# A decode block on one core: TensorE's loop from seven turns over two places of 64 KB to nine turns over three places of 32 KB

## The chip, the core and the metric

The kernel runs on one core of a Trainium2 chip. A core has five engines that run side by side and meet only at semaphores: TensorE (PE in the profile) multiplies matrices, VectorE (DVE), ScalarE (ACT) and GpSimd (POOL) do the work between the products, and SyncE (SP) here only issues transfers. Sixteen DMA engines move data from the chip's memory (HBM) to the core's own memory (SBUF: 128 partitions); products come out in PSUM, in eight banks. The metric is the device time of one execution in microseconds (us), less is better.

## What is computed

One decode step of a transformer block, in float32, for 8 sequences of one token each: attention over the last 1024 positions of a cache, then a gated MLP. Cut to what matters (`layernorm` has no gain; `B_x` is not used):

```python
x = A_x                                              # (8, 1, 1024)
q = layernorm(x) @ wq                                # 32 heads of 128; wq is 1024 x 4096
k, v = the last W = 1024 rows of k_cache, v_cache    # (8, 4 heads, 1024, 128), each for 8 query heads
p = softmax(q k^T / sqrt(128))
h = x + (p v) @ wo                                   # wo is 4096 x 1024
g, u = layernorm(h) @ w_gate, layernorm(h) @ w_up    # 1024 x 3584
out = h + (gelu(g) * u) @ w_down                     # 3584 x 1024
```

Every weight and every cached row is used once, so 111 MB have to come from HBM for some 0.1 MB of activations.

## The kernel before

The weights and the cache are packed ahead of the launch so that each transfer reads one long row for each of the 128 partitions. They come as 13 **passes** (`PASSES`, line 25): `q0 q1` (the query projection), `k0 v0 k1 v1` (keys and values of sequences 0 to 3 and 4 to 7), `o0 o1` (output projection), `g0 u0 g1 u1` (gate and up projection, in a part of 2048 and one of 1536 columns) and `d0` (16 of the 28 row chunks of the down projection). A full pass is 16384 words for each partition, 64 KB; `g1` and `u1` have 12288.

SBUF tile `w` has two **places** of 64 KB (`HALF`), and pass *i* goes to place *i* mod 2. `load` (line 225) issues the transfers on SP's queue, in the passes' order. The transfer of a pass waits until TensorE is through with the pass two before it, which had the same place, so while one pass is multiplied the next one is on its way. `d0` comes as two transfers of 32 KB. Behind it come the 12 remaining row chunks of the down projection, in transfers of 7, 2 and 2 chunks (`PARTS`; 4096 bytes a chunk and partition) and the last chunk cut into 640 and 384 words.

TensorE runs a real loop of seven turns (lines 168 to 182). A turn holds a pass from place 0 (`one_pass(0)`), eight transposes of `p_sb` (the softmax; in most turns their result is not used), and a pass from place 1; the last turn holds `d0` alone. In a pass a chunk `c` of 128 rows is multiplied by four products, one for each 32 columns of the array (line 161): the stationary operand is a 128 x 32 piece of `st[s]` (activations, 1024 columns a place), the moving one 128 x 512 words of `w`. Chunks 0 to 3 add up in one PSUM bank, 4 to 7 in the next. The profile has two records for each of these products. Behind the loop stand 16 products for 8 row chunks of the down projection (line 202), 12 for the next three (line 209), and 8 for the last chunk (line 217).

Between the passes the other engines fold the partial sums, run the softmax and the norms, and write the activations of the next pass into `st`. TensorE waits for a transfer (`s_la`, `s_lh`, `s_lb`) and for an activation (`s_ta`, `s_tb`) with separate semaphores. VectorE's whole program is recorded and then put in a block that is run once; ScalarE, GpSimd and SP run straight through. The order of everything is the order in which it is written.

Of the kernel before, what the change touches and what calls it, by code (L numbers as in the profile page):

```python
# [4 lines left out]
AF = mybir.ActivationFunctionType  # L5
# [3 lines left out]
P = 128  # L9
# [11 lines left out]
HALF = 16384  # L21
# [5 lines left out]
PASSES = ("q0", "q1", "k0", "v0", "k1", "v1", "o0", "o1", "g0", "u0", "g1", "u1", "d0")  # L27
TURNS = 7

FIRST = 16  # L30
PARTS = (7, 2, 2)

QUADS = 24
# [74 lines left out]
def decode_block(nc, out, x, srcs, W):  # L108
# [3 lines left out]
    def sb(name, shape):  # L112
# [9 lines left out]
    s_x0, s_x, s_la, s_lh, s_lb, s_ta, s_tb, s_p, s_at, s_id = [  # L122
        nc.alloc_semaphore("s_" + n) for n in ("x0", "x", "la", "lh", "lb", "ta", "tb", "p", "at", "id")]
# [4 lines left out]

    w = sb("w", [P, 2 * HALF])
    st = [sb(f"st{s}", [P, D + 32]) for s in range(2)]  # L130
    p_sb = sb("p", [P, W])
    ident = sb("ident", [P, P])
    at_ = sb("at", [P, DF // P, 32])
# [10 lines left out]
    tail_at = []  # L144
    at = HALF
    for n in PARTS:
        tail_at.append(at)
        at += n * D
    last_at = at
# [5 lines left out]
    def one_pass(s):  # L155
        for c in range(NC):
            if s == 0 and c == 4:
                take(s_lh, 16)
            for j in range(NQ):
                at = s * HALF + ((c // 4 * NQ + j) * 4 + c % 4) * N  # L160
                ins = nc.tensor.matmul(  # L161
                    bank(2 * s + c // 4)[32 * j:32 * j + 32, :],
                    st[s][:, (c * NQ + j) * 32:(c * NQ + j + 1) * 32], w[:, at:at + N],
                    start=(c % 4 == 0), stop=(c % 4 == 3))
        ins.then_inc(pe.sem, 1)

    nc.tensor.wait_ge(s_id, 1)
    with nc.Fori(0, TURNS, 1, engines=on_pe, hint_back_edge=True) as turn:
        take(s_la, 16)
        take(s_ta, 1)  # L170
        one_pass(0)
        with nc.tensor.If(turn < TURNS - 1):
            take(s_p, 1)
            for h in range(2):
                for i in range(KC // 2):
                    c = h * KC // 2 + i
                    ins = nc.tensor.transpose(pp[h][:, i], p_sb[:, c * P:(c + 1) * P], ident)  # L177
                ins.then_inc(pe.sem, 1)
            take(s_lb, 16)
            take(s_tb, 2)  # L180
            one_pass(1)

    def done(name):
        t, s = divmod(PASSES.index(name), 2)
        return (pe.sem, 4 * t + (4 if s else 1))

    def turned(t, h):
        return (pe.sem, 4 * t + 2 + h)

    pe.n = 4 * (TURNS - 1) + 1  # L190

    rows = DF // P
    place, of = [], []
    for i, n in enumerate(PARTS):
        for k in range(n):
            place.append(tail_at[i] + k * D)
            of.append((s_dn[i], 16))
    for q in range(FIRST, QUADS):
        for ch in range(2):
            r = 2 * (q % 2) + ch  # L200
            at = place[q - FIRST] + ch * N
            ins = pe(lambda e: e.matmul(  # L202
                bank(6)[32 * r:32 * r + 32, :], at_[:, q, :], w[:, at:at + N],
                start=(q < FIRST + 2), stop=(q >= QUADS - 2)), of[q - FIRST], (s_at, 1), inc=False)
    t_pairs = pe.mark(ins)
    for q in range(QUADS, rows - 1):
        for j in range(NQ):
            at = place[q - FIRST] + j * QW
            ins = pe(lambda e: e.matmul(  # L209
                bank(7)[32 * j:32 * j + 32, 0:QW], at_[:, q, :], w[:, at:at + QW],  # L210
                start=(q == QUADS), stop=(q == rows - 2)), of[q - FIRST], inc=False)
# [37 lines left out]
    for name in PASSES[:-2]:  # L249
        next_load(name)  # L250
# [320 lines left out]
```

## Time and profile before

| | us |
|---|---|
| time, median of 3 runs | 265.15 (265.07 to 265.83) |
| the profiled execution, its own time | 265.19 |
| its span, from the first to the last instruction | 263.9 |
| outside the span | 1.3 |
| TensorE busy | 132.7 |
| VectorE, ScalarE, GpSimd busy | 37.3, 19.1, 4.4 |
| read from HBM | 111.18 MB, 422 GB/s over the span |

The profile is of one execution. Times are counted from the start of the span. A share of the DMA engines is that of all 16, and a row of short stretch can read above 1, since a packet's whole time is put to where it starts. "PEclk" is TensorE's granted clock: 1.00 is 2.4 GHz, 0.50 is 1.2 GHz.

### The profile page before, as it was taken

Reading aid. Unit: us, or ns where it says so; the run is one execution under the profiler, and the core shown is the slowest. Engines: PE = TensorE matmul, PEld = TensorE weight load, DVE = VectorE, ACT = ScalarE, POOL = GpSimd, SP = SyncE. Lnnn points to the kernel's source line nnn. Section 1 sums busy time; section 2 is a strip of 40 time slices with the busy share of each in tenths; the row PEclk is TensorE's granted clock in tenths of the full one; section 3 lists DMA queues with packets and bytes.
Section 4 is the critical chain, followed back from the end, with each engine's and each line's share of the span. In section 5 each row is a group of like instructions: output and inputs, shape, how many; then the busy total and the mean of one; then the engine's idle time right before and its main releaser. Section 6 shows DMA issues by size and latency. Waiting matters only on the chain. (4 is left out here: it accounts for less than half of the span.)

```text
span 263.9 us, 2184 instructions
## 1 busy us (share of the span) xinstructions
PE 132.7 (50%) x952; PEld 41.6 (16%) x952; DVE 37.3 (14%) x105; ACT 19.1 (7%) x28; POOL 4.4 (2%) x11
## 2 busy tenths in 40 slices
PE   0004905806826507618608509409509187683766
PEld 0001301201222102112102202002203022220222
DVE  0060110120120200120220100540100301012013
ACT  1030000000020000100000000210300002010000
POOL 2000100000000000000000000000000001000000
PEclk9999975985956965975957956956968959799579
DMA  8997999999899979998998999799989989999993
GB/s 318 482 457 338 477 477 397 397 477 467 348 457 477 457 338 477 477 407 387 477 477 358 437 477 457 338 477 477 447 375 410 477 380 454 397 467 407 417 422 137
DMA packets 3073, 111.33 MB, mean 422 GB/s; under 512 B 480, under 2 KB 768, under 8 KB 896
## 3 DMA queue, kind: packets, MB, share of 16 engines
q1 hardware_dynamic: 2880, 111.20, 97.9%
q10 hardware_dynamic: 192, 0.11, 0.1%
q8 instruction: 1, 0.02, 0.0%
HBM read 111.18 MB, written 0.13 MB: 422 GB/s over the span
## 5 line engine op out<-in xcount | busy, mean ns | idle before, releaser
L161 PE MATMUL banks<-w,st 128*32 128x512 f32 x832 | 118.4, 731 | 120.3 <-PEq L153 120.3
L161 PEld LDWEIGHTS banks<-w,st 128*32 128x32 f32 x832 | 33.0, 131 | 200.7 <-issue 200.7
L177 PE MATMUL banks<-ident,p 128*128 128x128 f32 x48 | 7.4, 303 | 6.3 <-PEq L153 6.3
L177 PEld LDWEIGHTS banks<-ident,p 128*128 128x128 f32 x48 | 5.8, 154 | 11.5 <-issue 11.5
L354 ACT ACTIVATE p<-banks,nmax 128x1024 f32<-128x1024 f32 x2 | 2.2, 1114 | 73.3 <-DVE nmax L90 73.3
L90 DVE TENSOR_REDUCE nmax<-banks 128x1 f32<-128x1024 f32 x2 | 2.4, 1224 | 33.9 <-PE banks L161 33.9
L90 DVE TENSOR_TENSOR y_sum<-y_sum,banks 128x512 f32<-128x512 f32 (+1 forms) x4 | 2.1, 552 | 33.0 <-PE banks L161 18.1
L202 PE MATMUL banks<-w,at 128*32 128x512 f32 x32 | 5.3, 829 | 2.1 <-DMA w<-weights 2.1
L90 DVE TENSOR_SCALAR q<-banks 128x512 f32<-128x512 f32 x2 | 1.4, 692 | 31.1 <-PE banks L161 31.1
L90 DVE TENSOR_TENSOR us<-us,banks 128x512 f32<-128x512 f32 (+1 forms) x2 | 1.4, 685 | 30.4 <-ACT us L409 17.5
L90 DVE TENSOR_TENSOR o_sum<-o_sum,banks 128x512 f32<-128x512 f32 x2 | 1.4, 688 | 30.0 <-ACT o_sum L370 30.0
L90 DVE TENSOR_TENSOR gs<-gs,banks 128x512 f32<-128x512 f32 (+1 forms) x2 | 1.4, 686 | 27.5 <-ACT gs L412 14.2
L90 DVE TENSOR_TENSOR d_sum<-d_sum,banks 128x256 f32<-128x256 f32 (+1 forms) x3 | 1.4, 507 | 19.0 <-ACT d_sum L442 13.4
L370 ACT COPY o_sum<-banks 128x512 f32<-128x512 f32 x2 | 1.2, 585 | 27.7 <-PE banks L161 27.7
L409 ACT COPY gs<-banks 128x512 f32<-128x512 f32 (+1 forms) x2 | 1.2, 583 | 27.4 <-PE banks L161 27.4
L409 ACT COPY us<-banks 128x512 f32<-128x512 f32 (+1 forms) x2 | 1.2, 583 | 26.7 <-PE banks L161 26.7
L286 ACT ACT_TABLE_LOAD x2 | 2.6, 1283 | 1.9 <-DVE x_sb L90 1.9
L390 POOL COPY y_ex<-y_sum 64x256 f32<-64x256 f32 x1 | 0.4, 391 | 136.2 <-DVE y_sum L90 136.2
L202 PEld LDWEIGHTS banks<-w,at 128*32 128x32 f32 x32 | 1.6, 143 | 6.0 <-issue 6.0
L309 ACT COPY st<-ln_t 128x1024 f32<-128x1024 f32 x2 | 2.1, 1046 | 5.1 <-DVE ln_t L90 5.1
L90 DVE STREAM_TRANSPOSE at<-hm 32x128 f32<-32x128 f32 (+2 forms) x5 | 2.2, 440 | 0.1
L90 DVE SCALAR_TENSOR_TENSOR o<-o_sum,share,o 128x128 f32<-128x128 f32 x6 | 2.1, 352 | 0.2
(59 smaller groups left out, 38.3 us busy)
## 6 DMA issues: line engine op xcount, KB each, us to landing
w<-weights SPq DMA_DIRECT2D x2, 6144.0 KB, 22.1
w<-weights SPq DMA_DIRECT2D x2, 4096.0 KB, 18.9
w<-weights SPq DMA_DIRECT2D x1, 3584.0 KB, 18.8
w<-weights SPq DMA_DIRECT2D x2, 1024.0 KB, 22.5
w<-weights SPq DMA_DIRECT2D x1, 320.0 KB, 24.2
w<-weights SPq DMA_DIRECT2D x1, 192.0 KB, 24.2
w<-weights SPq DMA_DIRECT2D x10, 29.3
out<-o_fin ACTq DMA_DIRECT2D x1, 80.0 KB, 1.6
```

Source lines behind the costliest of these rows:

```text
L90: ins = getattr(self.eng, n.name)(*n.args, **n.kw)
L161: ins = nc.tensor.matmul(bank(2 * s + c // 4)[32 * j:32 * j + 32, :], st[s][:, (c * NQ + j) * 32:(c * NQ + j + 1) * 32], w[:, at:at + N], ...
L177: ins = nc.tensor.transpose(pp[h][:, i], p_sb[:, c * P:(c + 1) * P], ident)
L202: ins = pe(lambda e: e.matmul(bank(6)[32 * r:32 * r + 32, :], at_[:, q, :], w[:, at:at + N], start=(q < FIRST + 2), stop=(q >= QUADS - 2)) ...
L286: t = act(lambda e: e.activation(sd, ve, AF.Sqrt), t_ve)
L309: nc.scalar.copy(to[1], wide).then_inc(s_tb, 2)
L354: t = act(lambda e: e.activation(p_sb, bank(0, 2), AF.Exp, bias=nmax, accum_out=tot), t)
L370: t = dve(lambda e: e.tensor_add(o_sum, o_sum, bank(3)), act(lambda e: e.copy(o_sum, bank(2)), done(f"v{hb}")))
L390: t1 = pool(lambda e: e.tensor_copy(ex[64:P], far[0:64]), t)
L409: t = act(lambda e: e.copy(out[:nb], bank(b)[:nb]), ready)
```

## The change

The 13 passes become 27 **units** (`UNITS`) of four chunks each: what was one pass is now part 0 and part 1, and `d0` has three parts, that is 24 of the 28 row chunks. `w` has three places of 32 KB (`RING`, `UNIT`), and unit *u* goes to place *u* mod 3. The transfer of unit *u* waits for the products of unit *u* - 3. The loop has nine turns of three units, 48 products, with the eight transposes between the first and the second unit in every turn, and no branch inside. The four row chunks behind the loop have places of their own; they come in transfers of 2 and 1 chunks and, as before, 640 and 384 words.

One semaphore for each place (`s_in`) now counts both the 16 increments of a transfer and one "token" of the engine that filled `st`. `st` has three tiles of 512 columns. The order of the units isn't that of the passes everywhere: `k1` part 0 comes before `v0`, part 1 behind it (its first scores are put aside in `s1`), and `g1` part 0 comes before `u0` part 1. GpSimd takes over the clearing of `x_sb`, two additions and the copies for `d0`.

```diff
+UNITS = (
+    ("q0", 0), ("q0", 1), ("q1", 0),
+    ("q1", 1), ("k0", 0), ("k0", 1),
+    ("k1", 0), ("v0", 0), ("v0", 1),
+    ("k1", 1), ("v1", 0), ("v1", 1),
+    ("o0", 0), ("o0", 1), ("o1", 0),
+    ("o1", 1), ("g0", 0), ("g0", 1),
+    ("u0", 0), ("g1", 0), ("u0", 1),
+    ("g1", 1), ("u1", 0), ("u1", 1),
+    ("d0", 0), ("d0", 1), ("d0", 2),
+)
+RING = 3
+TURNS = len(UNITS) // RING
+UNIT = 4 * NQ * N
...
-PARTS = (7, 2, 2)
-
-QUADS = 24
+PAIRED = 24
+PARTS = (2, 1)
...
+    def unit(p):
+        take(s_in[p], 17)
+        for c in range(4):
+            if p == RING - 1 and c == 2:
+                take(s_half, 16)
             for j in range(NQ):
...
+    with nc.Fori(0, TURNS, 1, engines=on_pe, hint_back_edge=True):
+        unit(0)
+        take(s_p, 1)
+        for h in range(2):
+            for i in range(KC // 2):
+                c = h * KC // 2 + i
+                ins = nc.tensor.transpose(pp[h][:, i], p_sb[:, c * P:(c + 1) * P], ident)
+            ins.then_inc(pe.sem, 1)
+        unit(1)
+        unit(2)
...
+    def load(u):
+        p = u % RING
+        if u >= RING:
+            sp.wait(count(u - RING))
+        to = w[:, p * UNIT:(p + 1) * UNIT]
+        src = srcs[u]
+        if u == len(UNITS) - 1:
+            for k, sem in enumerate((s_in[p], s_half)):
+                n = UNIT // 2
+                nc.sync.dma_start(to[:, k * n:(k + 1) * n], src[:, k * n:(k + 1) * n]).then_inc(sem, 16)
             return
         n = src.shape[1]
...
+        if p == RING - 1 and n < UNIT:
+            to = to.rearrange("p (h n) -> p h n", h=2)[:, :, 0:n // 2]
+            src = src.rearrange("p (h n) -> p h n", h=2)
+        else:
+            to = to[:, 0:n]
+        nc.sync.dma_start(to, src).then_inc(s_in[p], 16)
...
+        if hb == 0:
+            scores, ready = bank(at_unit("k0", 0) % RING, 2), done("k0", 1)
+        else:
+            scores, ready = s1, act(lambda e: e.copy(s1[:, N:2 * N], bank(0)), done("k1", 1))
...
+    t = dve(lambda e: e.tensor_add(y_sum, y_sum, bank(1)), t, done("o0", 1))
+    t = dve(lambda e: e.tensor_add(y_sum, y_sum, bank(2)), t, done("o1", 0))
     h_sb = sb("h_sb", [P, QW])
...
+    t_h = folded("y", y_sum, (t, done("o1", 1)), h_sb, bank(0))
+    normed_in = layernorm_t(h_sb, "ln2", t_h)
+    normed_in(dve, "g0", 0)
+    normed_in(act, "g0", 1)
+    normed_in(act, "u0", 0)
...
+    t = pool(lambda e: e.tensor_add(d_sum[:, 0:QW], d_sum[:, 0:QW], h_sb), t)
+    t = dve(lambda e: e.tensor_add(d_sum, d_sum, bank(1)), t, done("d0", 1))
     pre = sb("pre", [P, QW])
...
+    t = folded("d", d_sum, (t, done("d0", 2)), pre, bank(2))
     t_pre = dve(lambda e: e.tensor_add(pre, pre, bank(7)[:, 0:QW]), t, t_quads)
```

How the instructions stand, first on TensorE from the last branch of the loop on. `s_dn0` to `s_dn4` are the transfers of the last row chunks, in their order; 32x512 is one product of 512 columns. Before:

```order
L168 COMPARE_AND_BRANCH
L202 MATMUL banks<-w,at 32x512 [waits s_dn0,s_at]
L202 MATMUL banks<-w,at 32x512 x13
L202 MATMUL banks<-w,at 32x512 [waits s_dn1]
L202 MATMUL banks<-w,at 32x512
L209 MATMUL banks<-w,at 32x256 x4
L209 MATMUL banks<-w,at 32x256 [waits s_dn2]
L209 MATMUL banks<-w,at 32x256 x7
L217 MATMUL banks<-w,at 32x160 [waits s_dn3]
L217 MATMUL banks<-w,at 32x160 x3
L217 MATMUL banks<-w,at 32x96 [waits s_dn4]
L217 MATMUL banks<-w,at 32x96 x3
```

And now, from the last unit of a turn on:

```order
L175 MATMUL banks<-w,st 32x512 [waits s_in2]
L175 MATMUL banks<-w,st 32x512 x7
L175 MATMUL banks<-w,st 32x512 [waits s_half]
L175 MATMUL banks<-w,st 32x512 x7
L181 REGISTER_ALU
L181 COMPARE_AND_BRANCH
L222 MATMUL banks<-w,at 32x256 [waits s_dn0]
L222 MATMUL banks<-w,at 32x256 x7
L222 MATMUL banks<-w,at 32x256 [waits s_dn1]
L222 MATMUL banks<-w,at 32x256 x3
L230 MATMUL banks<-w,at 32x160 [waits s_dn2]
L230 MATMUL banks<-w,at 32x160 x3
```

Behind the loop there are 36 products before and 20 now (the last four, of 96 columns, are cut off here); behind the third transfer from the end stand eight products of 256 columns before, four now.

On SP's queue stand the transfers of the weights; 128x16384 is 64 KB for each partition, `s_pe` the count of finished products. Before, from the third transfer on:

```order
L237 DMA w<-weights 128x16384 [waits s_pe] x8
L237 DMA w<-weights 128x12288 [waits s_pe] x2
L233 DMA w<-weights 128x8192 [waits s_pe]
L233 DMA w<-weights 128x8192
L258 DMA w<-weights 128x7168 [waits s_pe]
L258 DMA w<-weights 128x2048 x2
L258 DMA w<-weights 128x640
L258 DMA w<-weights 128x384
```

And now, from the fourth on:

```order
L255 DMA w<-weights 128x8192 [waits s_pe] x16
L255 DMA w<-weights 128x6144 [waits s_pe]
L255 DMA w<-weights 128x8192 [waits s_pe]
L255 DMA w<-weights 128x6144 [waits s_pe] x2
L255 DMA w<-weights 128x2x3072 [waits s_pe]
L255 DMA w<-weights 128x8192 [waits s_pe] x2
L247 DMA w<-weights 128x4096 [waits s_pe]
L247 DMA w<-weights 128x4096
L265 DMA w<-weights 128x2048
L265 DMA w<-weights 128x1024
L265 DMA w<-weights 128x640
L265 DMA w<-weights 128x384
```

With the first ones, that are not shown, 19 transfers become 32, of the same words in all, and the transfers of the last chunks no longer have a wait of their own.

## Rows read from the trace of the kernel before

**Rows 1.** The page: span, busy time by engine, and the weights' DMA queue.

```profile
span 263.9 us, 2184 instructions
...
PE 132.7 (50%) x952; PEld 41.6 (16%) x952; DVE 37.3 (14%) x105; ACT 19.1 (7%) x28; POOL 4.4 (2%) x11
...
q1 hardware_dynamic: 2880, 111.20, 97.9%
```

**Rows 2.** TensorE's timeline: start, us from start to end, line, shape, records [idle before].

```profile
23.15 8.49 PE L161 MATMUL banks<-w,st 128*32 128x512 f32 x64 [23.15 <-PEq L153]
...
61.84 9.62 PE L161 MATMUL banks<-w,st 128*32 128x512 f32 x64 [10.29 <-PEq L153]
...
177.95 9.59 PE L161 MATMUL banks<-w,st 128*32 128x512 f32 x64 [10.32 <-PEq L153]
...
197.30 8.45 PE L161 MATMUL banks<-w,st 128*32 128x512 f32 x64 [8.74 <-PEq L153]
211.83 9.71 PE L161 MATMUL banks<-w,st 128*32 128x512 f32 x64 [6.08 <-PEq L153]
...
226.36 8.77 PE L161 MATMUL banks<-w,st 128*32 128x512 f32 x64 [3.79 <-PEq L153]
236.07 3.64 PE L161 MATMUL banks<-w,st 128*32 128x512 f32 x32 [0.94 <-PEq L153]
245.64 6.44 PE L161 MATMUL banks<-w,st 128*32 128x512 f32 x32 [5.93 <-PEq L153]
254.16 5.34 PE L202 MATMUL banks<-w,at 128*32 128x512 f32 x32 [2.08 <-DMA w<-weights]
...
260.10 1.07 PE L209 MATMUL banks<-w,at 128*32 128x256 f32 x16 [0.18 <-DMA w<-weights]
260.99 0.62 PE L217 MATMUL banks<-w,at 128*32 128x160 f32 x16
```

**Rows 3.** The chain that ended last, its last pieces: start, us, what.

```profile
236.03 24.03 DMA w<-weights
...
260.10 1.11 PE banks L209 x16
...
261.24 0.43 DVE pre L90
...
261.93 0.25 DVE o_fin L90
```

**Rows 4.** The DMA view of 257.5 to 258.0: queue, packets, MB, share of 16 engines.

```profile
q8 instruction: 1, 0.02, 13.4%
```

**Rows 5.** Stretches of the tail: busy (count) by engine, PEclk, DMA share, GB/s.

```profile
254.00:256.00 2.00, 1.84 (x12) 0.61 (x16) 0.00 (x0) 0.00 (x0) 0.00 (x0) 0.69 1.02 426
256.00:258.00 2.00, 2.00 (x16) 0.72 (x12) 0.00 (x0) 0.00 (x0) 0.00 (x0) 0.50 1.00 411
258.00:259.00 1.00, 1.00 (x16) 0.40 (x12) 0.00 (x0) 0.00 (x0) 0.00 (x0) 0.92 0.96 370
259.00:260.00 1.00, 0.93 (x16) 0.17 (x6) 0.45 (x2) 0.00 (x0) 0.00 (x0) 1.00 0.36 126
260.00:261.00 1.00, 0.90 (x18) 0.56 (x21) 0.73 (x2) 0.41 (x1) 0.40 (x1) 1.00 0.05 17
```

**Rows 6.** VectorE's timeline: the second softmax, and the fold and norm behind `o1`.

```profile
109.65 1.23 DVE L90 TENSOR_REDUCE nmax<-banks 128x1 f32<-128x1024 f32 x1 [16.77 <-PE banks L161]
...
113.46 0.69 DVE L90 COPY st<-banks 128x512 f32<-128x512 f32 x1 [0.55 <-PE banks L177]
...
167.69 1.47 DVE L90 TENSOR_TENSOR y_sum<-y_sum,banks 128x512 f32<-128x512 f32 x3 [18.15 <-PE banks L161]
...
174.26 0.69 DVE L90 COPY st<-ln_t 128x1024 f32<-128x1024 f32 x1
```

**Rows 7.** The DMA view: issue of the second part of the output, KB, us to landing.

```profile
out<-o_fin SPq DMA_DIRECT2D x1, 48.0 KB, 1.6
```

More of the change, by code (lines that the diff above doesn't have):

```diff
@@ L165, in one_pass @@
         ins.then_inc(pe.sem, 1)
[L167 to L181, printed above, removed]
@@ L194, in decode_block, with count, done, turned @@
+    def count(u):
+        t, p = divmod(u, RING)
+        return (pe.sem, 5 * t + (1, 4, 5)[p])
+    def done(name, part):
+        return count(UNITS.index((name, part)))
+    def turned(u, h):
+        return (pe.sem, 5 * (u // RING) + 2 + h)
+    def token(u, ins):
+        ins.then_inc(s_in[u % RING], 1)
+    def at_unit(name, part):
+        return UNITS.index((name, part))
+    pe.n = 5 * TURNS
+    at = RING * UNIT
+    tail_at, place, of = [], [], []
     for i, n in enumerate(PARTS):
+        tail_at.append(at)
@@ L195, in decode_block @@
         for k in range(n):
-            place.append(tail_at[i] + k * D)
+            place.append(at + k * D)
             of.append((s_dn[i], 16))
[L198 to L201, printed above, removed]
+        at += n * D
+    for q in range(PAIRED, rows - 1):
+        for j in range(NQ):
+            k = place[q - PAIRED] + j * QW
             ins = pe(lambda e: e.matmul(
-                bank(6)[32 * r:32 * r + 32, :], at_[:, q, :], w[:, at:at + N],
-                start=(q < FIRST + 2), stop=(q >= QUADS - 2)), of[q - FIRST], (s_at, 1), inc=False)
@@ L205, in decode_block @@
[L205 to L211, printed above, removed]
+                bank(7)[32 * j:32 * j + 32, 0:QW], at_[:, q, :], w[:, k:k + QW],
+                start=(q == PAIRED), stop=(q == rows - 2)), of[q - PAIRED], inc=False)
@@ new lines, in queries_in @@
+    def queries_in(name, part):
+        u, hb = at_unit(name, part), int(name[1])
+        to = st[u % RING][:, 0:HB * 136].rearrange("p (b n) -> p b n", b=HB)
+        for hf in range(2):
+            ins = dve(lambda e: e.tensor_copy(
+                to[:, :, 64 * hf:64 * hf + 64].rearrange("p b (r n) -> p b r n", r=2)[:, :, :, 0:REP],
+                qt[hf][:, :, HB * hb:HB * hb + HB, 0].rearrange("p (r h) b -> p b r h", r=2)),
+                t_qt, t_zero[u % RING], inc=False)
+        token(u, ins)
@@ new lines, in decode_block, with lower, upper, let @@
+    gs, us, ge, hm = [[sb(f"{n}{k}", [P, N]) for k in range(2)] for n in ("gs", "us", "ge", "hm")]
+    def lower(out, name):
+        return act(lambda e: e.copy(out[:nb], bank_of(name, 0)[:nb]), done(name, 0))
+    def upper(out, name, t):
+        return dve(lambda e: e.tensor_add(out[:nb], out[:nb], bank_of(name, 1)[:nb]), t, done(name, 1))
+    def let(name, part, *deps):
+        for d in deps[:-1]:
+            pool.wait(d)
+        token(at_unit(name, part), nc.gpsimd.wait_ge(*deps[-1]))
@@ L441, in decode_block @@
+    chunks_in(1, t_u1)
+    t_us = upper(us[1], "u1", t_u1)
+    t = dve(lambda e: e.tensor_mul(hm[1][:nb], ge[1][:nb], us[1][:nb]), t_ge, t_us)
+    n = (rows - FIRST) * 32
+    t = dve(lambda e: e.transpose(at_[0:nb, FIRST:rows].rearrange("p c m -> p (c m)"), hm[1][:nb, 0:n]), t)
+    for j in range(NQ - 1):
+        c = FIRST + 4 * j
+        t = dve(lambda e: e.transpose(
+            at_[nb:P, c:c + 4].rearrange("p c m -> p (c m)"), hm[1][32 * j:32 * j + 32, n:N]))
+    chunks_in(2, t)
     d_sum = sb("d_sum", [P, N])
-    t = act(lambda e: e.copy(d_sum, bank(0)), done("d0"))
```

276 lines of the change are left out of this document (115 added, 161 removed).

## The prediction

> **What bounds the kernel now.** I read the page first: the span is 263.9 us, TensorE is busy for half of it, and the one queue that brings the weights fills the 16 DMA engines for 97.9% [rows 1]. Then TensorE's timeline: from pass to pass its bursts start 19.35 us apart (61.84 to 177.95 is 116.11 us for six passes), whatever the burst itself takes, and before each it has been idle for 4 to 10 us [rows 2]. So the transfers set the pace, and a burst starts when its data land. Last the chain that ended last: 24.03 us of DMA up to 260.06, then 1.11 us of products, VectorE's additions to 262.18, and the output [rows 3]. The end is thus the landing of the third transfer from the end, at 260.06, plus 3.8 us.
>
> How did that landing come so late? One packet of 0.02 MB on an "instruction" queue starts between 257.5 and 258.0 and takes 13.4% of 16 engines over 0.5 us, that is 1.07 us on one engine [rows 4]. In the stretch 259 to 260 the DMA share is 0.36, and in 260 to 261 it is 0.05, less than one engine of 16 [rows 5]. One engine, I read, finishes about a microsecond behind the others, and a transfer counts as landed only when its last part is there: without the fetch the 260.06 would be 258.99.
>
> **The change part by part.** *Bytes*: the same words, so the stream's bulk doesn't move. *Number of transfers*: 19 become 32, and one of these has two pieces for each partition, so I count 14 more. The price of one is in the timeline: a 64 KB pass takes 19.35 us, a 32 KB half (226.36 to 236.07) takes 9.71, and twice 9.71 is 19.42 [rows 2]. The difference, 0.07 us, is what an additional transfer costs in a full queue; the 48 KB pass (211.83 to 226.36, 14.53 us) agrees, being 0.02 above three quarters of 19.35. Start times are good to about 0.02, so the price lies between 0.05 and 0.09: 14 x 0.07 = **+1.0 us** (0.7 to 1.3), all of it on the path, since nothing hides a stream that is always full.
>
> *Is it always full?* A load now waits for the products of the unit three before it, while two units (2 x 9.7 us) are still queued. The longest burst of 32 records, a unit's count, took 6.44 us [rows 2]. So from the landing of a unit to the issue of its successor pass some 6.5 us of 19.4. The longest chain between units is the second softmax: `k1` part 1 ends, scores are copied (0.7 us, as VectorE's copy of 512 columns), then from maximum to the filled `st` 109.65 to 114.15, 4.5 us [rows 6]. `v1` part 0 then starts 6.44 + 5.2 = 11.6 us after `k1` part 1 landed, 1.9 us later than its data, and ends at 18; the queue holds data up to 29. The fold and norm behind `o1` take 167.69 to 174.95, 7.3 us [rows 6], and one addition of them now comes earlier: `g0` starts at 13.7 at most, ends at 20.2, against the same 29. Even if the first product started as late as now, at 23.15 [rows 2], its unit would end at 29.6, and the first three units land at 23.15 + 9.7 = 32.9. All edits on VectorE, ScalarE and GpSimd, the reordered units, the moved clearing of `x_sb` and the eight transposes in two more turns lie under this cover and cost nothing; without it they would cost what they overrun.
>
> *The fetch.* Between 254 and 259 no engine but TensorE has an instruction: VectorE, ScalarE and GpSimd wait for its products [rows 5], SP for the end. So I take the fetch to be TensorE's. Behind the loop it now has 20 products instead of 36, in the whole code 76 instead of 108; at the time of the fetch it was amid the first 16 [rows 2]. The shorter program is likely to end before the place that called for more code. Then **-1.07 us** at the landing. The Trainium skill (Runtime: NRT & Kernel Launch, Instruction fetch mechanics) says that an engine's instruction memory is refilled in blocks of 16 KiB, 256 instructions; the 0.02 MB of the row agree. By that rule the fetch belongs to a place in the code and not to the end of the loop, and would go; the page doesn't say where the place is, and no run here shows it yet.
>
> *The tail.* The third landing from the end comes at 258.99 + 1.0 = 260.0; the last one 1024 words later (1.2 us and two prices of 0.07) at 261.3. Now TensorE: `L202` got its data at 254.16 with 5120 words a partition still to come; the last half of `d0` part 2 lands with 4096 to come, 1.2 us + 1.0 later, at 256.35; the two chunks behind it at 258.85. Its 16 records take 1.8 us at the pace of the quick burst (3.64 for 32), 2.7 at that of `L202` (5.34 for 32), 3.2 at that of the slowest (6.44 for 32) [rows 2]; these are mostly matters of the clock, which fell to 0.50 in 256 to 258 after a pause of 2.08 us [rows 2, 5], and such a pause stands here again. I take `L202`'s pace: end at 259.05. Then 16 records of 256 columns: 1.07 us [rows 2] at full clock, twice that at half; I take 1.6, to 260.65. Then eight more, 0.6, to **261.3** (260.7 all fast, 262.8 all slow), where the chain of before has 261.21. VectorE and the output follow as before. With all fast the last products end at 261.3 + 0.3, and the last addition (0.25) at 261.9 instead of 262.18 [rows 3].
>
> *Sum*, on the profiled execution's 265.19 (the median is 265.15): 261.3 against 261.21, **265.3**; all fast -0.3, 264.9; up to +0.6 where the clock is half for some of it, 265.8.
>
> **The rivals.** *The fetch stays* (slower). It may come with the end of a hinted loop, which both kernels have. For it: the hint is the same; against it: before, it came 5 us behind the loop's last burst. The place is the tail, the price 1.07 us. Then the third landing from the end is 261.05, the last 262.4, the last products end at 262.7 and the last addition at 263.0 instead of 262.18: 266.0. It decides at whatever time a fetch comes behind the first load, since the engine that serves it has no pause to catch up in.
> *TensorE at half clock bounds the tail* (slower): 262.8 instead of 261.21, 266.8; for it the 0.50 in rows 5, against it the 0.92 of the stretch behind, with TensorE at work.
> *An additional transfer costs nothing* when the next is queued anyway: then everything lands 1.0 earlier, the products end at 260.3 and the kernel at 264.3. The 0.07 speak against it.
> *The stream runs dry*: a chain would have to be 9 us longer than in rows 6; an overrun of 2 us gives 267.3.
> *Each additional transfer shows its whole latency*: the smallest takes 1.6 us from issue to landing [rows 7]; 13 x 1.6 is 20.8 in place of the 1.0, so 285. The rows of passes and halves speak against it, as transfers stand in line. The Trainium skill (SBUF — State Buffer, The DMA setup-cost knee) puts a fixed 2 us or so on every transfer and advises the largest ones that fit; 13 of those would be an estimated 26 us; the trace's 0.07 us disagrees for queued ones.
>
> **How the numbers follow.** Forecast 0.55; the fetch stays 0.26; half clock 0.09; free transfers 0.07; dry 0.02; whole latencies 0.01. A measurement of this kernel can tell about 0.3% from no change, 0.8 us: same is 264.35 to 265.95. Faster: half of the free transfers and a little of the forecast, 0.06. Slower: most of the fetch's 266.0 (0.16), half clock 0.08, the last two 0.03, a little of the forecast 0.02, so 0.29. Same is 0.65. The range 264.6 to 266.3 holds the forecast, nearly all of the fetch and the milder half clocks.
>
> **What would show it.** Right: bursts of 32 records 9.7 us apart from `q1` to `o1`; the weights' queue at 97% or more; no instruction packet in the last 10 us; one DMA landing ahead of the `L222` products near 260.0, and the chain ending with them. Wrong: a stretch with a DMA share clearly below 1 before 258 (dry); an instruction packet in the tail and a share of 0.05 again in the last microsecond (fetch); units 9.68 apart and a tail that starts 1 us earlier (free); `L222` idle for nothing and PEclk 0.50 up to 261 (half clock).

## Result

| | before | after |
|---|---|---|
| time, median of 5 runs each | 265.24 (265.07 to 265.83) | 266.46 (266.38 to 266.61) |
| the profiled execution, its own time | 265.19 | 266.61 |
| its span | 263.9 | 265.3 |

After to before is 1.0044 [1.0029, 1.0058]: slower by 1.2 us. The forecast was 265.3, "same", with a range up to 266.3; the time lies 0.16 us above that range.

The page of the changed kernel (the lines that [rows 1] showed of before; the last line is the instruction queue):

```profile
span 265.3 us, 2255 instructions
...
PE 147.0 (55%) x976; PEld 45.9 (17%) x976; DVE 36.0 (14%) x100; ACT 20.5 (8%) x32; POOL 7.6 (3%) x18
...
q1 hardware_dynamic: 4880, 111.20, 97.9%
...
q8 instruction: 1, 0.02, 0.0%
```

The stream is as full as before, 97.9%. TensorE's timeline of the changed kernel (columns as in [rows 2]), three units and the one behind the second softmax, then the tail:

```profile
81.29 5.25 PE L175 MATMUL banks<-w,st 128*32 128x512 f32 x32 [3.70 <-PEq L166]
91.00 5.34 PE L175 MATMUL banks<-w,st 128*32 128x512 f32 x32 [4.46 <-PEq L166]
100.72 5.34 PE L175 MATMUL banks<-w,st 128*32 128x512 f32 x32 [4.38 <-PEq L166]
...
111.87 5.32 PE L175 MATMUL banks<-w,st 128*32 128x512 f32 x32
```

```profile
246.57 3.64 PE L175 MATMUL banks<-w,st 128*32 128x512 f32 x32 [2.72 <-PEq L166]
251.46 1.92 PE L175 MATMUL banks<-w,st 128*32 128x512 f32 x16 [1.25 <-PEq L166]
256.37 1.92 PE L175 MATMUL banks<-w,st 128*32 128x512 f32 x16 [2.98 <-PEq L166]
258.77 1.07 PE L222 MATMUL banks<-w,at 128*32 128x256 f32 x16 [0.48 <-DMA w<-weights]
260.05 0.64 PE L222 MATMUL banks<-w,at 128*32 128x256 f32 x8 [0.21 <-DMA w<-weights]
262.45 0.79 PE L230 MATMUL banks<-w,at 128*32 128x160 f32 x16 [1.76 <-DMA w<-weights]
```

Units start 9.71 us apart. The unit behind the softmax starts 11.15 us after the one ahead of it, so 1.4 us later than the pace, and the stream goes on. In the tail TensorE is done with all that has landed by 260.7 and then waits 1.76 us for the transfer of 640 words. The chain that ended last (start, us, what) names it too:

```profile
234.33 28.08 DMA w<-weights
...
262.45 0.52 PE banks L230 x8
...
263.06 0.49 DVE o_fin L107 x2
```

Where [rows 3] had 24.03 us of DMA up to 260.06 and 3.8 us behind it, there now are 28.08 us up to 262.41 and 2.9 us behind. What the DMA engines did in these last microseconds, first the DMA view of 260 to 261 (queue, packets, MB, share of 16 engines), then the stretches, columns as in [rows 5]:

```profile
q8 instruction: 1, 0.02, 6.8%
```

```profile
259.00:260.00 1.00, 0.84 (x16) 0.26 (x8) 0.53 (x2) 0.21 (x1) 0.23 (x1) 1.00 1.03 395
260.00:261.00 1.00, 0.64 (x8) 0.16 (x8) 0.24 (x1) 0.00 (x0) 0.00 (x0) 1.00 0.52 180
261.00:262.00 1.00, 0.00 (x0) 0.00 (x0) 0.18 (x1) 0.00 (x0) 0.00 (x0) 1.00 0.05 7
262.00:263.00 1.00, 0.55 (x16) 0.29 (x16) 0.00 (x0) 0.00 (x0) 0.00 (x0) 1.00 0.02 8
```

The packet of [rows 4] is still there: 0.02 MB, 6.8% of 16 engines for 1 us, that is 1.09 us on one engine. Before, it started 257.5 to 258.0; now it starts after 260, among the last transfers. The share of 0.05 in 261 to 262 is again less than one engine of 16: fifteen are done, one is not. The clock is 1.00 in all these rows and costs nothing here.

### The profile page after: what moved, and what is told of

Same layout as the page of the kernel before. It is cut to its first block, busy times and chain, and to the rows that moved or that the text cites. A ratio compares the mean times of both kernels' runs of the same rounds, so it can differ in the third digit from the quotient of the medians.

```text
span 265.3 us, 2255 instructions
## 1 busy us (share of the span) xinstructions
PE 147.0 (55%) x976; PEld 45.9 (17%) x976; DVE 36.0 (14%) x100; ACT 20.5 (8%) x32; POOL 7.6 (3%) x18
## 3 DMA queue, kind: packets, MB, share of 16 engines
q1 hardware_dynamic: 4880, 111.20, 97.9%
## 5 line engine op out<-in xcount | busy, mean ns | idle before, releaser
L175 PE MATMUL banks<-w,st 128*32 128x512 f32 x864 | 134.4, 777 | 109.9 <-PEq L166 109.9
L175 PEld LDWEIGHTS banks<-w,st 128*32 128x32 f32 x864 | 36.6, 137 | 200.2 <-issue 200.2
L187 PE MATMUL banks<-ident,p 128*128 128x128 f32 x72 | 10.7, 296 | 3.8 <-PEq L166 3.8
L187 PEld LDWEIGHTS banks<-ident,p 128*128 128x128 f32 x72 | 8.4, 150 | 12.2 <-issue 12.2
L320 ACT COPY st<-ln_t 128x512 f32<-128x512 f32 x6 | 3.5, 618 | 17.3 <-DVE q L107 12.3
L479 POOL COPY st<-at 128x512 f32<-128x512 f32 x3 | 1.8, 610 | 69.1 <-DVE gs L107 51.6
L107 DVE TENSOR_REDUCE nmax<-banks 128x1 f32<-128x1024 f32 x1 | 1.2, 1225 | 17.4 <-PE banks L175 17.4
L107 DVE COPY st<-ot 128x64 f32<-128x64 f32 x8 | 1.8, 287 | 9.4 <-ACT y_sum L413 9.4
L343 POOL MEMSET st<- 128x544 f32 x3 | 1.7, 551 | 44.1 <-PE banks L175 44.1
L107 DVE COPY st<-banks 128x512 f32<-128x512 f32 x2 | 1.4, 692 | 7.1 <-PE banks L187 7.1
## 6 DMA issues: line engine op xcount, KB each, us to landing
w<-weights SPq DMA_DIRECT2D x1, 320.0 KB, 28.1
```

Source lines behind the costliest of these rows:

```text
L107: ins = getattr(self.eng, n.name)(*n.args, **n.kw)
L175: ins = nc.tensor.matmul(bank(p)[32 * j:32 * j + 32, :], st[p][:, (c * NQ + j) * 32:(c * NQ + j + 1) * 32], w[:, at:at + N], start=(c == 0 ...
L320: lambda e: e.copy(to, src) if eng is act else e.tensor_copy(to, src), t, *deps, inc=False))
L343: t_zero = {u % RING: pool(lambda e: e.memset(st[u % RING], 0.0), count(u)) for u in (1, 2, 3)}
L479: token(u, nc.gpsimd.tensor_copy(st[u % RING][:, 0:N].rearrange("p (c x m) -> p c x m", c=8, x=2), at_[:, 8 * part:8 * part + 8].unsqueeze ...
```

## Experiments

What each was to tell: what an additional transfer costs (first run), what calls for the packet (next eleven), and whether the packet alone holds the end (last six). In all of them "after" is the changed kernel, and the ratio is to runs of the kernel before on the same chip.

### The price of a transfer

Each unit's transfer in two, 59 instead of 32:

```diff
-        nc.sync.dma_start(to, src).then_inc(s_in[p], 16)
+        for h in range(2):
+            nc.sync.dma_start(to[:, h], src[:, h]).then_inc(s_in[p], 16)
```

> The changed kernel with every load of a unit issued as two transfers of half its columns: 59 transfers instead of 32, the same words. The price of the prediction, 0.07 us for one more transfer in a full queue: 27 x 0.07 = 1.9 us more, 268.4. The rival that a queued transfer costs nothing: 266.5. That each shows its latency of 1.6 us or so: over 300.

Measured: 268.56 us (268.34 to 268.79, two runs), with the packet in the tail as in after. That is 2.1 above after's 266.46 for 27 more transfers, **0.078 us each**. The term of the forecast (0.07, from pass against two halves) holds; 14 of them are 1.1 us.

### What calls for the packet: the loop's hint, VectorE, the place of the loop in the code

Leaving out the hint at the loop's end; writing the ninth turn out behind a loop of eight; VectorE's program without its block:

```diff
-    with nc.Fori(0, TURNS, 1, engines=on_pe, hint_back_edge=True):
+    with nc.Fori(0, TURNS, 1, engines=on_pe, hint_back_edge=False):
```

> The changed kernel with the hint on the loop's back edge taken away; nothing else. In the changed kernel one 16 KB instruction packet stands in the tail (its window 260.4 to 260.6), and the last two transfers land 1.5 us later than 15 of their 16 parts. Theory A (the packet is asked for when TensorE leaves its hinted loop): without the hint it is gone from the tail; if the loop's turns ask for code instead, such packets are spread over the run, and one engine is late by about 1.1 us for each that it serves. Without any: the last transfer lands at 261.5, the span is 263.9 and the time 265.2. Theory B (the packet belongs to a place in the code behind the loop, whatever the hint): it stays in the tail, time 266.5 within 0.2.

```diff
+    with nc.Fori(0, TURNS - 1, 1, engines=on_pe, hint_back_edge=True):
+        one_turn()
+    one_turn()
```

> The changed kernel with a loop of eight turns and the ninth written out behind it: the same products in the same order, but TensorE leaves the loop some 29 us earlier. Theory A (asked for at the exit): the instruction packet moves to about 230 us; the engine that serves it stays about 1.1 us behind to the end, so the last transfers land 1.1 us late instead of 1.5: 266.0. Theory B (a place in the code behind the loop): the code behind the loop is now 48 products longer, so the packet comes at another time that the number of instructions sets, not the exit; were it still near 260, the time would be 266.5.

```diff
-    with nc.body("once", valid_engines=on_dve):
...
-        vector.put()
+    vector.put()
```

> The changed kernel with VectorE's program written straight, not as a block with a hinted branch back that is run once. Theory C (the instruction packet in the tail is VectorE's): it is gone from the tail, or comes at another time, and the time is 265.2 without it. Theories A and B (TensorE's): a packet stays at 260.4 to 260.6; VectorE may ask for one of its own at some earlier time, and then another engine is late by about 1.1 us too: 266.5 to 267.0.

Measured: 266.17 (265.49 to 266.49), 266.53 (266.26 to 266.88) and 266.57 (266.54 to 266.7). The packet stays in all three, at 260 to 261, 261 to 262 and 260 to 261. So it is not the exit of a hinted loop and not VectorE's. VectorE's plain program has a packet of its own, 8 KB on another queue at 114.1 us, that its block kept away. With the ninth turn written out there are two 16 KB packets, the first near 250 us: it is TensorE's code that counts, and in this run more of it in a straight line brought a second packet.

Then the loop's first instruction was put at a chosen place of the code, 0 or 100 for after, 64 or 0 for before:

```diff
+                 head_slot={nc.tensor.engine: 0}):
```

> The changed kernel with the first instruction of TensorE's loop placed at slot 0 of a code block, by padding that is jumped over; the same work. TensorE's program has 305 instructions (built size), the loop 215, and the first eight products behind it end at instruction 256 counted from slot 0 of this placement within a few. Theory D (the 16 KB packet depends on where TensorE's code lies in its blocks): the tail still crosses into the second block, in the middle of the products of 256 columns, so a packet comes in the tail again, perhaps some tenths of a us earlier or later than 260.5: 266.4. Theory E (it comes a fixed way before the program's end, wherever the code lies): at 260.5 as in the changed kernel, 266.5.

> The changed kernel with the first instruction of TensorE's loop at slot 100 of a code block: the loop lies in slots 100 to 315, so it crosses into the second block in each turn, and the code behind the loop, 316 to 398, crosses no boundary of 256. Theory D (a packet is asked for when TensorE enters a block for the first time behind the loop): none in the tail; the last transfer lands at 261.5, the span is 263.9, the time 265.2. If a packet is asked for in the loop instead, one early in the run, it leaves one engine 1.1 us late: 266.1. Theory E (a fixed way before the program's end): 260.5 again, 266.5.

> The kernel before with the first instruction of TensorE's loop at slot 64 of a code block; nothing else. The loop then lies in slots 64 to 345, the code behind it in 348 to 496, with no boundary of 256 in it. Theory D: no packet in the tail; the third transfer from the end lands at 259.0 instead of 260.1, the last at 260.4, and TensorE's products, at half clock before, become the end: 264.5, 0.7 less than before. Theory E: nothing changes, 265.2.

> The kernel before with the first instruction of TensorE's loop at slot 0 of a code block: the loop lies in 0 to 282, the code behind it in 284 to 432. Theory D in its form 'entering a block': no boundary in the tail either, so 264.5, as with slot 64. If the packet depends on something else in the placement than a crossing of 256, this and slot 64 differ. Theory E: 265.2.

Measured: 266.59, 266.34, 266.07 and 265.97, none clearly below its own kernel (266.34, of runs from 265.91 to 266.46, against after's 266.46). The packet of the tail stayed in each (261 to 262, 260 to 261, 259 to 260, 256 to 259), so the rule by the place in blocks of 256 falls in the form in which it was put; and 266.07 and 265.97 are not the 265.2 of the other theory either, though the intervals of their ratios, 1.0026 [0.9999, 1.0053] and 1.0013 [0.9973, 1.0054], still hold no change. Three of the four (place 0 and both of before) got a second packet, within the first 8 us. The DMA view of after with place 0, 0 to 6 us:

```profile
q8 instruction: 1, 0.02, 1.0%
```

That engine was late for the rest of the program: the second unit starts at 24.38 (first row) against 23.01 in after, and the second half of the last unit at 257.75 (second row) against 256.37, 1.38 us, 250 us behind the packet. With place 100, which had no such packet, the two start at 22.96 and 256.31, so it isn't the placing as such.

```profile
24.38 3.64 PE L175 MATMUL banks<-w,st 128*32 128x512 f32 x32 [2.73 <-PEq L166]
...
257.75 3.13 PE L175 MATMUL banks<-w,st 128*32 128x512 f32 x16 [2.74 <-PEq L166]
260.58 2.08 PE L223 MATMUL banks<-w,at 128*32 128x256 f32 x24
262.45 0.65 PE L231 MATMUL banks<-w,at 128*32 128x160 f32 x16
```

### More code behind the loop, and less

Products of one column behind the last ones, 18 in after and 17 in before:

```diff
+    for _ in range(18):
+        nc.tensor.matmul(bank(6)[0:32, 0:1], at_[:, 0, :], w[:, at - 1:at], start=True, stop=True)
```

> The changed kernel with 18 products of one column (72 more TensorE instructions) behind its last ones, into a PSUM bank that nobody reads any more; the output does not depend on them. In every run so far the 16 KB instruction packet starts 1.0 to 1.5 us after TensorE has passed the wait for the transfer whose products lie some 82 instructions ahead of the program's end. Theory F, the packet is called for at a place counted from the end of TensorE's program: with 72 more instructions behind it that place is reached only once the last weights are there, so the packet starts at 263 us or later and delays none of them; the last weights land at 261.5, the span is 263.8 and the time 265.2 (between 264.9 and 265.5). Theory G, the place is counted from the start of TensorE's program, or belongs to the exit of the loop: the packet starts at 260.3 to 260.7 as before, the last weights land at 263.0 and the time is 266.5 (266.2 to 266.8). The added products take perhaps 2 us on TensorE, while VectorE's last sums and the stores run, and should not set the end in either case; if they do, the span ends with TensorE.

> The kernel before with 17 products of one column (68 more TensorE instructions) behind its last ones, into a bank that nobody reads any more; the output does not depend on them. Theory F (the place is counted from the end of the program): the packet, which started at 258.1 and put the last weights from 260.5 to 261.4, starts behind 260.5 and delays none of them or only the last by some tenths: time 264.2 to 264.6, about 0.9 below the kernel before, and it would be the fastest version so far. Theory G (from the start, or the loop's exit): packet at 258.1, time 265.2, the same as before. If both this and the run on the changed kernel go by F, the difference between the two, 1.0 us, is the price of 14 more transfers alone.

Measured: 266.22 (265.01 to 266.68) and 266.40 (265.98 to 266.95). The packets stay at 260 to 261 and at 257 to 258: a place counted from the program's end is out. Before now has a second one, between 262 and 263, and it meets the output. The DMA view of that run (KB, us from issue to landing; [rows 7] had 1.6 for the same line):

```profile
out<-o_fin SPq DMA_DIRECT2D x1, 48.0 KB, 2.8
```

In after's run the late part is that of the very last transfer; TensorE has the 640 words at 261.08 and waits 1.27 us for the other 384:

```profile
261.08 0.48 PE L230 MATMUL banks<-w,at 128*32 128x160 f32 x8 [0.19 <-DMA w<-weights]
262.83 0.37 PE L230 MATMUL banks<-w,at 128*32 128x96 f32 x8 [1.27 <-DMA w<-weights]
```

The other way, one product kept for each of the last transfers, 4 of 20 in after and 5 of 36 in before:

```diff
-        for j in range(NQ):
+        for j in range(1 if q in (PAIRED, rows - 2) else 0):
             k = place[q - PAIRED] + j * QW
```

> The changed kernel with one product kept for each of the transfers behind the loop's own, four of 20 (down projection incomplete; the tail's sums read a cleared bank); every transfer and its wait stay. TensorE's program gets 64 instructions shorter. The run with more instructions behind kept one packet at the same place, so the place is not counted from the end. Theory H: TensorE calls for the packet when its code passes a place counted from the start, some way behind the loop, and this program ends before it: the trace has no 16 KB instruction packet, the last weights land with the others at 261.5, one and a half microsecond earlier than in the changed kernel, and the time is 264.9 (264.6 to 265.2), of which up to 0.3 is the shorter work behind the last weights. Theory I, the packet belongs to leaving the loop, whatever follows: it starts at 260.3 to 260.9, the last weights land at 262.8 to 263.1, time 266.1 to 266.4.

> The kernel before with one product kept for each of its five transfers behind the loop (down projection incomplete, sums read cleared banks); every transfer and its wait stay. TensorE's program is 124 instructions shorter. Theory H, a place counted from the start: the packet of the kernel before started 1.4 us after TensorE had passed the wait for the second of these transfers, some 35 to 50 instructions behind the loop, and this program ends 21 behind the loop: no packet, the last weights land with the others at 260.5, time 263.9 to 264.4. Theory I, leaving the loop: packet within 253 to 258.5, last weights at 261.4, time 264.9 to 265.2. The difference between this run and its pair on the changed kernel is then the price of the 14 further transfers with no packet in either (H), or with one in both (I): 1.0 either way.

Measured: 266.0 (265.35 to 267.15), span 264.1, and **264.18** (264.04 to 264.86), span 262.7, ratio 0.9964 [0.9954, 0.9973]. In neither is there a packet while weights come. The transfer of 640 words, KB and us from issue to landing, in the run on before, and the piece of its last chain (start, us, what) that ends with the third landing from the end:

```profile
w<-weights SPq DMA_DIRECT2D x1, 320.0 KB, 23.3
...
235.86 22.94 DMA w<-weights
```

The profile of before has 24.2 for the 640 words: the packet made them 0.9 us late there. The third landing from the end comes at 258.80 instead of 260.06; the prediction read 258.99 for it. Without the packet before is 1.06 us faster, but 31 of its 36 products behind the loop are missing, too; the next section has the kernel with all of them. On after the same edit takes 1.2 us off the span but only 0.5 off the time: the packet now comes at 265.4, behind the span, and what lies outside the span grew from 1.3 to 2.0 us. The expected 264.9 was missed by that and by some 0.5 us in the span, whose end TensorE's products hold and not the weights: the loop's last 16 records took 3.56 us, at a clock of 0.54 from 256.0 to 258.4.

### Without the packet, with all the work

TensorE's code behind the loop in a block that is run once and ends in a hinted branch back, not taken (as VectorE's has it):

```diff
+    nc.br("tail", engines=on_pe)
+    with nc.body("tail", valid_engines=on_pe):
+        back = nc.tensor.mark_branch_hint_location()
...
+        nc.tensor.br_lt(tail, 1, on_true="tail", on_false="tail_end").branch_hint(back)
+    nc.switch_bb("tail_end")
```

> The changed kernel with TensorE's code behind the loop put into a block of its own that is run once and ends in a hinted branch back that is not taken (the form that VectorE's code already has; there, taking it away brought an 8 KB instruction packet at 114.4 us that no other run has). All work stays. Theory H1, the hint keeps the following code from being called for: no 16 KB packet before the last weights are there, they land together at 261.5, the span is 263.8 and the time 265.0 to 265.3, the same as the kernel before. Theory H2, passing the place in the code calls for the packet with or without a hint: packet at 260.3 to 261, last weights at 263.0, time 266.3 to 266.6.

> The same block put around the code behind the loop of the kernel before. All work stays. H1: no packet before the last weights, which land together at 260.4; with the products behind them as in the kernel before the span is 262.8 to 263.0 and the time 264.1 to 264.5, faster than the kernel before by 0.8 to 1.1. H2: packet at 258.1, last weights at 261.4, time 265.2. If H1 holds in both, the difference between the pair, 0.9 to 1.0 us, is the 14 further transfers alone.

Measured: 266.76 (266.73 to 266.94) and 266.19 (265.41 to 267.19). On after the packet is gone altogether; the transfer of 640 words takes

```profile
w<-weights SPq DMA_DIRECT2D x1, 320.0 KB, 26.5
```

against 28.1 in after, 1.6 us less, and the time is no better. TensorE's timeline and three stretches of this run show why:

```profile
256.53 3.64 PE L175 MATMUL banks<-w,st 128*32 128x512 f32 x16 [2.97 <-PEq L166]
259.92 2.73 PE L227 MATMUL banks<-w,at 128*32 128x256 f32 x24
262.47 0.62 PE L235 MATMUL banks<-w,at 128*32 128x160 f32 x16
```

```profile
258.00:259.00 1.00, 1.00 (x8) 0.22 (x4) 0.00 (x0) 0.00 (x0) 0.00 (x0) 0.50 1.00 404
...
260.00:261.00 1.00, 1.00 (x16) 0.59 (x12) 0.75 (x2) 0.31 (x1) 0.28 (x1) 0.50 0.57 208
261.00:262.00 1.00, 1.00 (x15) 0.45 (x8) 0.42 (x1) 0.09 (x1) 0.11 (x1) 0.50 0.00 0
```

From 261 on no weights move, and TensorE is busy without a pause until 263.1. Its granted clock is 0.50, the 1.2 GHz level, up to 262: the loop's last 16 records take 3.64 us instead of the 1.92 of after. That is the rival "half clock" of the prediction, at its price: 266.8.

On before the packet is only moved, to between 262 and 263, and the output's line reads `48.0 KB, 2.9` in place of 1.6. Nor was there much to lose in this execution. The last piece of its chain is

```profile
261.74 0.25 DVE o_fin L90
```

where [rows 3] had 261.93, so with all the products the last addition ended only 0.2 us earlier. Its chain leads back over operations of VectorE and ScalarE to the 32 records behind the loop, 254.13 to 259.50 and in part at the clock 0.50, and not to the last weights. Two of the twelve executions have spans of 262.7 and 262.6, 1.2 us below before's 263.9, but about 3.6 and 4.2 us outside them, and times of 266.3 and 266.85; there is no trace of these.

### Packet and clock apart

Eight extra products ahead of the wait for the second half of every third unit keep TensorE at work in the pause; with and without the block of the last section.

```diff
             if p == RING - 1 and c == 2:
+                for _ in range(8):
+                    nc.tensor.matmul(bank(6)[0:32, :], st[p][:, 0:32], w[:, block(p, 0, 0):block(p, 0, 0) + N],
+                                     start=True, stop=True)
                 take(s_half, 16)
```

> The changed kernel with TensorE's code behind the loop in the hinted block that took the packet away, and eight extra products of 512 columns ahead of the wait for the second half of every third unit (into a bank that nobody reads; the result is the same). They fill 1.9 us of the idle 3.0 us ahead of the loop's last 16 products. Theory K, the clock alone holds the end once the packet is gone: these products and those behind them run at 1.00, the last weights land at 261.5 to 261.7, the products behind them end at 262.0, and the time is 265.0 to 265.4, 1.4 us below the same kernel without the extra products. Theory L, something else holds the end: time 266.4 or more with the clock at 1.00. Should the 32 instructions more bring the packet back, the weights land at 263 and the time is 266.4.

> The changed kernel with the same extra products and without the hinted block. Theory K and the packet theory together: the clock is 1.00 in the tail, the packet comes at 260.4 to 260.9, the last weights land at 262.8 to 263.1 and the time is 266.2 to 266.5, as in the changed kernel; the difference to its pair, 1.0 to 1.4 us, is the packet alone at equal clock. If the packet is not what counts, the pair has equal times.

Measured: 269.85 (268.56 to 270.56) and 269.22 (268.17 to 269.51); this pair tells nothing of the question. All eight products went to the same quarter of TensorE's columns and ran one behind another. In the groups by line of the first (busy us, mean ns of a record):

```profile
L173 PE MATMUL banks<-w,st 128*32 128x512 f32 x144 | 66.2, 613 | 0.0
```

Spread over the four quarters, as the loop's own products are:

```diff
-                    nc.tensor.matmul(bank(6)[0:32, :], ...
+                    nc.tensor.matmul(bank(6)[32 * (i % NQ):32 * (i % NQ) + 32, :], ...
```

> The changed kernel with the hinted block behind the loop (no packet) and eight extra products of 512 columns, two in each quarter of the columns, ahead of the wait for the second half of every third unit: 1.9 us at clock 1.00, into a bank that nobody reads. Theory K, the clock alone holds the end once the packet is gone: the loop's last 16 products and those behind them run at 1.00, the last weights land at 261.5 to 261.7, and the time is 265.0 to 265.4, against 266.76 of the same kernel without the extra products. Theory L, something else: 266.4 or more at clock 1.00. The weights must not run dry for the run to count: the second half of the last unit has to land at 256.4 to 256.7.

> The changed kernel with the same eight products and no hinted block. If the packet still comes at 260.4 to 261 with the clock at 1.00, the last weights land at 262.8 to 263.1 and the time is 266.2 to 266.5; the difference to its pair, 1.0 to 1.4 us, is then the packet alone at equal clock. If the packet is not what counts, the pair has equal times.

Measured: **265.27** (264.88 to 266.82, 12 runs), ratio 1.0001 [0.9988, 1.0014], and **266.34** (265.15 to 266.72, 12 runs), ratio 1.0034 [1.0023, 1.0045]. TensorE's tail with the block:

```profile
253.43 1.93 PE L173 MATMUL banks<-w,st 128*32 128x512 f32 x16
256.61 1.92 PE L178 MATMUL banks<-w,st 128*32 128x512 f32 x16 [1.25 <-PEq L166]
259.01 1.07 PE L230 MATMUL banks<-w,at 128*32 128x256 f32 x16 [0.48 <-DMA w<-weights]
260.29 0.64 PE L230 MATMUL banks<-w,at 128*32 128x256 f32 x8 [0.21 <-DMA w<-weights]
261.14 0.80 PE L238 MATMUL banks<-w,at 128*32 128x160 f32 x16 [0.20 <-DMA w<-weights]
```

and without it, the last two pieces:

```profile
260.99 0.48 PE L233 MATMUL banks<-w,at 128*32 128x160 f32 x8 [0.20 <-DMA w<-weights]
262.73 0.37 PE L233 MATMUL banks<-w,at 128*32 128x96 f32 x8 [1.27 <-DMA w<-weights]
```

Both run at the clock 1.00 from 254 to 263. With the packet in the tail TensorE waits 1.27 us for its last weights; without it, 0.20. The pair differs by 1.07 us: **the packet, at equal clock**. In the traces TensorE's last products end at 261.94 and 263.10, 1.16 us apart. In the profiled execution with the block the packet came behind the weights (262 to 263) and met the output, and its time is 266.4; it is one of two in twelve with a span above 265, and the other ten have 263.6 to 263.9. That the packet delayed nothing in those ten is read from their spans; there is no trace of one. Of the twelve without the block one has a span of 263.8, too (265.15), so the place of the packet may differ between executions of one kernel.

The case with both delays is among the first runs: with VectorE's plain program the packet is there, and the clock in the tail is 0.50 from 258.7 to 260. From its timeline:

```profile
256.80 3.55 PE L175 MATMUL banks<-w,st 128*32 128x512 f32 x16 [2.98 <-PEq L166]
...
263.02 0.37 PE L230 MATMUL banks<-w,at 128*32 128x96 f32 x8 [1.04 <-DMA w<-weights]
```

All together (the clock is that of one execution each):

| after, with | packet among the last weights | clock in the profiled tail | us |
|---|---|---|---|
| nothing | yes | 1.00 | 266.46 |
| VectorE's plain program | yes | 0.50 | 266.57 |
| block | no | 0.50 | 266.76 |
| extra products | yes | 1.00 | 266.34 |
| both | no | 1.00 | 265.27 |

With the packet the time is 266.3 to 266.6 at either clock, with the half clock alone it is 266.76. Taking away one of the two delays gives nothing, taking away both gives 1.2 us.

## Why the prediction failed

**The stream's bound, and that it stays full: right.** 97.9%, units 9.71 us apart, one transfer's landing at the head of the last chain. The late starts of units (1.4 us behind the softmax) lie under the cover that was counted, and all edits on VectorE, ScalarE and GpSimd cost nothing that shows.

**14 more transfers at 0.07 us, +1.0: right.** The 27 more of the first run cost 0.078 each. The Trainium skill (SBUF — State Buffer, The DMA setup-cost knee) puts a fixed 2 us or so on every transfer, by which those 27 would cost an estimated 54 us; for queued ones the run disagrees and says 2.1.

**The packet goes away, -1.07: wrong, and this is the step that failed.** It was TensorE's, as the prediction had it from the idle engines; that is shown by the runs in which only TensorE's code changed and a packet came, went or moved. But "the shorter program is likely to end before the place that called for more code" was a guess about a place that no row showed. With twenty products in a straight line behind the loop the packet still comes among the last weights; with four it came only behind the span. So the stream's +1.0 came without the -1.07. The rival "the fetch stays", at 0.26, is what happened, and not for the reason given there: without the hint at the loop's end the packet came all the same.

**The size of that rival: too small by 0.46 us.** It said 266.0. It took the packet's delay of the last transfers to be the packet's own 1.07 us. The transfer of 640 words was 0.9 us late in before (24.2 against 23.3) and 1.6 us late in after (28.1 against 26.5). With the stream's 1.0 to 1.1 us and some 0.7 us of greater delay, less 0.3 to 0.4 us that by difference lie in the shorter work behind the last weights, this is the 1.4 us between the spans. The delay differed between runs of like kernels, too (1.3 us for the last transfer with the extra products, 1.5 in after). Part of it shows in the DMA views of after, of 261 to 262 and of 262 to 263 (queue, packets, MB, share of 16 engines):

```profile
q1 hardware_dynamic: 5, 0.01, 5.1%
...
q1 hardware_dynamic: 6, 0.01, 2.1%
```

In the microsecond behind the instruction packet the late engine's packets took 0.16 us each, in the next one 0.06. So it lost some 0.5 us (an estimate, 5 times 0.10) on top of the packet's 1.09. Why they were slow, and why the 640 words were only 0.9 us late in before, stays open.

**The half clock, 0.09: its chance was too small for what was forecast.** Its price was right to a tenth of a microsecond (266.8 against 266.76), and it came in the very case that the forecast assumed, packet gone and all else the same. In the changed kernel itself it does not show: its profile has the clock at 1.00 in the tail, and with the packet the weights are later than the products at 0.50, too (VectorE's plain program, 266.57). The forecast's own 265.3 came out (265.27) only with the packet gone and TensorE held at work besides. It mixed the two paces of the tail into one value, between 264.9 and 266.8. The loop's last 16 records took 1.92 us in after, 3.64 with the block, and 2.83 to 3.56 in six other runs on after whose clock changed meanwhile, and only the quick pace gave 265.3.

**It decides at whatever time a fetch comes, since a full engine can't catch up: right.** A packet at 4 us put the unit at the end back by 1.38 us. A packet in the tail cost 1.07 us, on a queue that is 97.9% full. Of instruction fetches the Trainium skill (Runtime: NRT & Kernel Launch, Instruction fetch mechanics) says that crossing a boundary of 16 KiB is mostly hidden. The size agrees with the packet's 0.02 MB; that it is hidden does not hold here, by those 1.07 us.

What stays open is the place that calls for the packet. It is not the exit of the hinted loop, not a count from the program's end, and not settled by the place of the loop's head in the code; short code behind the loop or a hinted block keeps it away or moves it. No complete version was faster than the kernel before. What the packet costs the kernel before is not shown: the 264.18 is without the packet but also without 31 products, the one profile with all of them gained 0.2 us ahead of the output, and every complete variant of before that was run put a packet on the weights or on the output in its profile.

## What to carry to other kernels

When a kernel is bound by a stream of transfers, count an instruction packet as one more transfer that the queue does not hide: look for it on the instruction queue, and don't book its disappearance as a gain unless a row shows what calls for it. When two delays end within a microsecond of each other (here the last weights and TensorE at half clock), undoing one can move nothing, so test them in all four combinations. Cutting a full stream into more transfers costs little each, 0.07 to 0.08 us here, but all of it is on the path.

## What the runs showed besides

- A packet behind the weights still costs: on the output it made a store of 48 KB land in 2.8 to 2.9 us instead of 1.6, and where it came behind the span the time outside was 2.0 us (one product for each transfer in after) and 2.3 us (the first run with extra products), instead of 1.3.
- Products in one quarter of TensorE's columns run one behind another: in the tail of that run fifteen records of the extra products took 6.60 us at the clock 1.00, where sixteen over the four quarters took 1.93.

```profile
255.22 6.60 PE L173 MATMUL banks<-w,st 128*32 128x512 f32 x15
```

- The clock of the tail was not the same in runs of nearly the same code: behind a pause of 2.98 us it read 1.00 in after and 0.50 with VectorE's plain program, behind one of 2.97 us it read 0.50 with the block. A pause of 1.25 us, with products in it, left it at 1.00.
